# Attention, expert routing and a cosine feed-forward in fp32: where the product's hi part is made, the order of the last two steps, and hints at conditional items

## The chip, the cores and the metric

One core of a Trainium2 chip runs the whole kernel. The time is the device time of one execution in microseconds. The kernel before took 1527.83 us (median of three runs, 1527.18 to 1529.36).

## The reference

Three stages, 4608 tokens of width 512. Attention over keys and values that are mean-pooled by 8; a router that sends each token to one of 8 experts (its two matrices 512x1024 and 1024x512, relu between, scaled by the gate); then a feed-forward for all tokens with one pair of matrices, 512x2048 and 2048x512. The part that the change touches most is the last:

```
def _moe2_ref(x, w_in, w_out):
    h = x @ w_in
    g = h * np.cos(h)
    return (g @ w_out).astype(np.float32)
```

## The kernel before

Matrix products keep fp32 accuracy with operands split in two: hi is the value rounded to the matmul's format, lo is the rest, and each product is the sum of three, hi by hi, lo by hi and hi by lo.

**Order.** Everything stands under a manual schedule: each engine does its instructions in the order in which the program lists them, and waits only for the data and buffers of each instruction.

**Expert items.** An expert's tokens are done in items of 512 (wide) or 256 (narrow). Five wide items are always there. Up to seven more wide ones and up to eight narrow ones depend on the routing: `more_wide(i)` opens `tc.If(nw > i)`, issues the item and nests the next one in it, `more_narrow(j)` does the same with `nn > j`. So each chain ends with one branch past the items that are not there, on every engine, after which an engine runs the code behind the chain. In the profile these branches are at L1037 and L1064. In an item `gemm1` (L788) makes eight blocks of 12 matmuls, in two PSUM banks by turns, each emptied by a relu on ScalarE (L791) and a lo part on VectorE (L792); `gemm2` (L803) makes the second product. Between them ScalarE (L127, `w_hi`) and GpSimd or VectorE (L130, `w_lo`) split the expert's weights. `t_x` (L773 to L776) transposes and splits the next item's x. SyncE loads weights and rows and stores the result (`y_store`, L811). The first narrow item also prepares the feed-forward (`prepare`): it loads and splits the first three weight tiles.

**Feed-forward.** 9 groups g of 512 tokens, 16 slices f of 128 hidden units: 144 steps n = 16 g + f. Step n lists, in this order:

- in group 0 only, for f up to 12: `f_split(n + 3)`, the split of the weight tile of three steps later, hi by ScalarE (L916), lo by GpSimd (L917); the load of the tile of six steps later;
- `ff1(n)`: 12 matmuls into one of three PSUM banks (L941);
- at f = 14 and 15: `x2_split`, half of the next group's x each, hi by ScalarE (L926), lo by GpSimd (L927);
- `ff2(n - 2)`: 12 matmuls (L965), into four banks that hold the group's output of 4 tiles of 128 tokens; after f = 15 `store`, four copies out of PSUM (L971 VectorE, L973 ScalarE) and then four scattered sends by GpSimd (L976);
- `act(n)`: h cos(h) from the bank of ff1(n). L949 on ScalarE scales h into u; L950 and L951 on VectorE take off whole turns (L950 reads and writes SBUF, L951 has two inputs in SBUF); L952 on ScalarE is the sine; L953 on VectorE multiplies u by h; L954 on VectorE makes the hi part, L955 on VectorE the lo part.

```
nc.vector.tensor_tensor(u, u, p, ALU.mult)
nc.vector.tensor_copy(gh, u)
nc.vector.tensor_tensor(gl, u, gh.bitcast(F32), ALU.subtract)
```

Here u lies in SBUF and p, the bank of ff1, in PSUM. u, gh and gl have two buffers each, by n % 2. The last two turns of the loop (n = 144 and 145) hold only ff2(142) and ff2(143), and then the last store.

Of the kernel before, what the change touches and what calls it, by code (L numbers as in the profile page):

```python
# [8 lines left out]
F32 = mybir.dt.float32  # L9
# [4 lines left out]
AF = mybir.ActivationFunctionType  # L14
ALU = mybir.AluOpType
# [4 lines left out]
ENGINES = ET.PE, ET.DVE, ET.SP, ET.Activation, ET.Pool  # L20
# [3 lines left out]
def attention_moe_ffn_kernel(  # L24
# [13 lines left out]
    nc = tc.nc  # L38
# [3 lines left out]
    NT, DM = out.shape  # L42
    E = w1.shape[0]
# [4 lines left out]
    FC2 = F2 // 128  # L48
# [3 lines left out]
    NW0, NWM = (NT - 256 * E + 511) // 512, (NT + 255 * E) // 512  # L52
# [16 lines left out]
    def bank(i, name):  # L69
        return psp[0].tile([128, 512], F32, tag=f"p{i}", name=name)  # L70
# [24 lines left out]
    POS = const.tile([128, NTILE], I32, name="POS")  # L95
# [15 lines left out]
    xr = [wap.tile([128, XW], F32, name=f"xr{r}") for r in range(4)]  # L111
# [20 lines left out]
    def apart(group, dma):  # L132

        tc.declare_no_dep(dma.ins, group=group, reason="disjoint rows")
        tc.add_to_no_dep_group(group, dma.ins)
# [601 lines left out]
    def experts_and_feed_forward():  # L737
# [79 lines left out]
        def item(i, w, conv=None, mid=None, when=None):  # L817

            n = w // 128
            w1c, w2c, on_dve, gates, txs, (at2, at1) = when  # L820
            if i:
                pos_store(i, w)
            for k in range(16):
                if k < 8:
                    gemm1(k, w)
                else:
                    gemm2(k // 2 - 4, k % 2, w)
                    for r in txs.get(k, ()):
                        t_x(r, n)
                if mid:  # L830
                    mid(k)
                for c in (w2c if k < 8 else w1c).get(k, ()):
                    w_hi(c)
                    w_lo(c, nc.vector if c in on_dve else nc.gpsimd)
                if k == at2:
                    fetch(tab, i + 1, 5, 1)
                if k == at1:
                    fetch(tab, i + 2, 5, 0)
                if conv:
                    conv(k)  # L840
                for r in gates.get(k, ()):
                    gate(r)
            x_load(tab, i + 2, n)
            y_store(i, w)
# [43 lines left out]
        def conv_part(i, k0, k1):  # L888

            if i >= len(PART):  # L890
                return None
            j0, n = sum(PART[:i]), 7 * PART[i]
            g = (x for j in range(j0, j0 + PART[i]) for x in conv_one(j))

            def some(k):
                for _ in range(n * (k - k0 + 1) // (k1 - k0) - n * (k - k0) // (k1 - k0) if k0 <= k < k1 else 0):
                    next(g)
            return some

        NG = NTILE // 4  # L900
# [4 lines left out]
        def wf(f, s, out):  # L905
            return WF[f][s][:, out * 512:(out + 1) * 512]
# [4 lines left out]
        def f_load(f):  # L911
            nc.sync.dma_start(stage(f), wd[:, f])

        def f_split(f, eng=nc.gpsimd):
            hi, lo = WF[f]
            nc.scalar.activation(hi, stage(f), AF.Copy)  # L916
            eng.tensor_tensor(lo, stage(f), hi.bitcast(F32), ALU.subtract)  # L917

        def x2_load(g):
            nc.sync.dma_start(craw[0].rearrange("p a (b n) -> p (a b) n", b=2), yv[:, :, g * 512:(g + 1) * 512])  # L920
            nc.sync.dma_start(POSF[:, g * 4:(g + 1) * 4], pv[0, g * 512:(g + 1) * 512].rearrange("(r p) -> p r", p=128))

        def x2_split(g, k):
            raw = craw[0][:, k, :].rearrange("p (b n) -> p b n", b=2)
            x, s, t = X2[g % 2], slice(k * 2, k * 2 + 2), slice(KC + k * 2, KC + k * 2 + 2)
            nc.scalar.activation(x[:, s, :], raw, AF.Copy)  # L926
            nc.gpsimd.tensor_tensor(x[:, t, :], raw, x[:, s, :].bitcast(F32), ALU.subtract)  # L927
            if k:
                nc.gpsimd.tensor_copy(POS[:, g * 4:(g + 1) * 4], POSF[:, g * 4:(g + 1) * 4])

        PH, G, O = {}, {}, {}
        GT2 = [XHI[:, 2 * i:2 * i + 2, :] for i in range(2)]

        def ff1(n):
            g, f = seq[n]
            x2 = X2[g % 2]
            p = bank((6, 1, 7)[n % 3], "ph2")
            c = 0
            for s, m in ((0, 0), (1, 0), (0, 1)):
                for kk in range(KC):  # L940
                    nc.tensor.matmul(p, wf(f, s, 0)[:, kk * 128:(kk + 1) * 128], x2[:, m * KC + kk, :], start=(c == 0), stop=(c == 3 * KC - 1))  # L941
                    c += 1
            PH[n] = p

        def act(n):
            p = PH.pop(n)
            u, nr = ys[:, n % 2, :], co[n % 2]
            gh, gl = GT2[n % 2][:, 0, :], GT2[n % 2][:, 1, :]
            nc.scalar.activation(u, p, AF.Identity, scale=1.0 / TWO_PI_EXACT, bias=quarter)  # L949
            nc.vector.tensor_scalar(nr, u, MAGIC, MAGIC, op0=ALU.add, op1=ALU.subtract)  # L950
            nc.vector.tensor_tensor(u, u, nr, ALU.subtract)  # L951
            nc.scalar.activation(u, u, AF.Sin, scale=TWO_PI)  # L952
            nc.vector.tensor_tensor(u, u, p, ALU.mult)  # L953
            nc.vector.tensor_copy(gh, u)  # L954
            nc.vector.tensor_tensor(gl, u, gh.bitcast(F32), ALU.subtract)  # L955
            G[n] = (gh, gl)

        def ff2(n):
            g, f = seq[n]
            gh, gl = G.pop(n)  # L960
            if f == 0:
                O[g] = [bank((0, 2, 3, 4)[r], "po") for r in range(4)]
            for r in range(4):
                for c, (a, s) in enumerate(((gh, 0), (gl, 0), (gh, 1))):
                    nc.tensor.matmul(O[g][r], a[:, r * 128:(r + 1) * 128], wf(f, s, 1), start=(f == 0 and c == 0), stop=(f == FC2 - 1 and c == 2))  # L965

        def store(g):
            os = [xr[r][:, 0:DM] for r in range(4)]
            for r, o in enumerate(os):
                if r % 2:  # L970
                    nc.vector.tensor_copy(o, O[g][r])  # L971
                else:
                    nc.scalar.activation(o, O[g][r], AF.Copy)  # L973
            for r, o in enumerate(os):
                nc.gpsimd.engine_nop()  # L975
                apart("out_rows", nc.gpsimd.indirect_dma_start(  # L976
                    out=out, out_offset=bass.IndirectOffsetOnAxis(ap=POS[:, g * 4 + r:g * 4 + r + 1], axis=0),
                    in_=o, in_offset=None,
                ))
            O.pop(g)  # L980

        class Bank:
            def __init__(self, p, at):
# [49 lines left out]
        nw = nc.values_load(tot[0:1, 0:1], engines=ENGINES, min_val=NW0, max_val=NWM)  # L1033
        nn = nc.values_load(tot[0:1, 1:2], engines=ENGINES, min_val=0, max_val=E)

        def more_wide(i):
            with tc.If(nw > i) as c:  # L1037
                item(i, 512, conv_part(i, 0, 16), None, WIDE)
                if i + 1 < NWM:
                    more_wide(i + 1)  # L1040
            if i < len(PART):
                with c.Else():
                    for j in range(i, len(PART)):
                        conv_part(j, 0, 1)(0)
# [16 lines left out]
                    f_load(f)  # L1061

        def more_narrow(j):
            with tc.If(nn > j) as c:  # L1064
                item(NROW + j, 256, None, None if j else prepare, NARROW)
                if j + 1 < E:
                    more_narrow(j + 1)
            if not j:
                with c.Else():
                    for k in range(16):  # L1070
                        prepare(k)

        more_wide(NW0)
        more_narrow(0)

        rawes.close()
# [3 lines left out]
        WF.append(tuple(XLO[:, 2 * i:2 * i + 2, :].rearrange("p a n -> p (a n)") for i in range(2)))  # L1080
        seq = [(g, f) for g in range(NG) for f in range(FC2)]
        NS = len(seq)
        for n in range(NS + 2):
            if n + 3 < FC2:
                f_split(n + 3)
                if n + 6 < FC2:
                    f_load(n + 6)
            if n < NS:
                g, f = seq[n]
                ff1(n)  # L1090
                if g + 1 < NG:
                    if f == 13:
                        x2_load(g + 1)
                    if f >= 14:
                        x2_split(g + 1, f - 14)
            if n >= 2:
                ff2(n - 2)
                if seq[n - 2][1] == FC2 - 1:
                    store(seq[n - 2][0])
            if n < NS:  # L1100
                act(n)

    with tc.manual_schedule():
        with ExitStack() as xes:
# [54 lines left out]
```

## Time and profile before

| | |
|---|---|
| median of three runs | 1527.83 us |
| the profiled execution | 1523.01 us |
| its span, first to last instruction | 1521.3 us |
| mean granted TensorE clock | 0.983 of 2.4 GHz |
| busy TensorE / VectorE / ScalarE / GpSimd | 1451.7 / 919.1 / 613.4 / 449.8 us |
| the first L941 of the feed-forward | at 718.91 us |

All times inside the kernel are counted from the first instruction of the profiled execution. In the timelines a row is one instruction, or several of one kind in a row; what ended an engine's idle time before it stands in brackets, with the length of that time. PE is TensorE, PEld its weight loads, DVE VectorE, ACT ScalarE, POOL GpSimd, SP SyncE; a q behind the name is the engine's sequencer. The tile names of the feed-forward are those of the buffers it took over: L955's `xhi<-ys,xhi` is gl from u and gh, `lo<-craw,hi` at L917 is the lo part of a weight tile.

### The profile page before, as it was taken

How to read it: one execution, taken by the hardware profiler on the slowest of the kernel's cores; microseconds unless marked ns; L12 is line 12 of the kernel's file. 1: busy time of each engine (PE TensorE's matmuls, PEld its weight loads, DVE VectorE, ACT ScalarE, POOL GpSimd, SP SyncE). 2: the span in 40 equal slices, each digit the busy share in tenths (PEclk: the TensorE clock that was granted, in tenths of full speed). 3: DMA queues.
4: the chain of work that ended last, by engine and by line, in shares of the span. 5: the costliest groups of instructions: out<-in, count | busy, mean ns of one | idle time of the engine just before them, and what ended most of it. 6: DMA issues, size and time to landing. Idle time of an engine off the chain costs nothing.

```text
span 1521.3 us, 20629 instructions
## 1 busy us (share of the span) xinstructions
PE 1451.7 (95%) x7526; PEld 1231.0 (81%) x7526; DVE 919.1 (60%) x1596; ACT 613.4 (40%) x1017; POOL 449.8 (30%) x340
## 2 busy tenths in 40 slices
PE   5999887999999998998999999999999999999997
PEld 4899766888888888998778888888888888888885
DVE  5788756676666532443787565655656565655653
ACT  5888633443443445664433232222223232222321
POOL 4668552443443533433432020110102010110201
PEclk9999889999999999999999999999999999999998
DMA  8765458667676654966221010000101000010000
GB/s 270 242 206 142 168 182 286 228 198 236 208 232 211 194 173 155 332 209 210 84 83 56 0 56 1 28 28 1 56 1 56 0 28 28 2 54 0 28 1 28
DMA packets 91327, 178.86 MB, mean 118 GB/s; under 512 B 15157, under 2 KB 34106, under 8 KB 91210
## 3 DMA queue, kind: packets, MB, share of 16 engines
q1 hardware_dynamic: 85290, 158.45, 32.7%
q0 software_dynamic: 5760, 18.92, 3.4%
q8 instruction: 63, 1.03, 0.3%
q14 instruction: 54, 0.44, 0.1%
q10 hardware_dynamic: 160, 0.02, 0.0%
HBM read 136.93 MB, written 40.44 MB: 117 GB/s over the span
## 4 chain that ended last, share of the span: by engine, by line
PE 42%; issue 5%; DVE 4%; ACT 1%; POOL 0%; DVEq 0%; POOLq 0%; ACTq 0%
PE ph L941 21%; PE po L965 21%; DVE xhi L955 2%; DVE ys L951 1%; DVE ys L953 1%; ACT ys L952 1%; POOL out_dram L976 0%; DVE xhi L954 0%; DVE co L950 0%; ACT ys L949 0%; DVEq L954 0%; POOLq L975 0%; DVEq L955 0%; POOLq L976 0%; POOLq L1154 0%
## 5 line engine op out<-in xcount | busy, mean ns | idle before, releaser
L130 POOL TENSOR_TENSOR lo<-raw,hi 128x1024 fp32r<-128x1024 f32 x83 | 200.1, 2416 | 289.8 <-ACT hi L127 243.0
L949 ACT ACTIVATE ys<-ph,quarter 128x512 f32<-128x512 f32 x144 | 99.0, 688 | 298.6 <-PE ph L941 298.6
L952 ACT ACTIVATE ys<-ys 128x512 f32<-128x512 f32 x144 | 91.0, 632 | 224.5 <-DVE ys L951 224.4
L965 PE MATMUL po<-hi,xhi 128*128 128x512 f32 x576 | 179.8, 391 | 0.2
L955 DVE TENSOR_TENSOR xhi<-ys,xhi 128x512 fp32r<-128x512 f32 x144 | 157.6, 1095 | 5.1
L953 DVE TENSOR_TENSOR ys<-ys,ph 128x512 f32<-128x512 f32 x144 | 99.1, 688 | 100.5 <-ACT ys L952 100.5
L950 DVE TENSOR_SCALAR co<-ys 128x512 f32<-128x512 f32 x144 | 61.1, 425 | 159.6 <-ACT ys L949 159.6
L965 PE MATMUL po<-fh,xhi 128*128 128x512 f32 x504 | 156.4, 390 | 1.0 <-DVE xhi L955 0.9
L803 PE MATMUL py<-ha,hi 128*128 128x256 f32 (+1 forms) x576 | 140.9, 337 | 0.0
L965 PEld LDWEIGHTS po<-hi,xhi 128*128 128x128 f32 x576 | 108.1, 188 | 25.9 <-DVE xhi L955 3.6
L127 ACT ACTIVATE hi<-raw 128x1024 fp32r<-128x1024 f32 x108 | 113.1, 1053 | 1.4 <-DMA raw<-in_moe_w_dram 0.9
L965 PEld LDWEIGHTS po<-fh,xhi 128*128 128x128 f32 x504 | 94.6, 188 | 22.2 <-DVE xhi L955 2.7
L965 PE MATMUL po<-lo,xhi 128*128 128x512 f32 x288 | 112.2, 390 | 0.0
L788 PE MATMUL ph<-xhi,hi 128*128 128x512 f32 (+1 forms) x416 | 97.4, 357 | 9.6 <-ACT xhi L775 5.1
L803 PEld LDWEIGHTS py<-ha,hi 128*128 128x128 f32 x576 | 96.7, 191 | 9.7
L951 DVE TENSOR_TENSOR ys<-ys,co 128x512 f32<-128x512 f32 x144 | 99.7, 692 | 5.0
L927 POOL TENSOR_TENSOR hb<-craw,hb 128x1024 fp32r<-128x1024 f32 x10 | 24.5, 2459 | 264.1 <-ACT hb L926 264.1
L965 PE MATMUL po<-fl,xhi 128*128 128x512 f32 x252 | 98.2, 390 | 0.0
L803 PE MATMUL py<-ha,lo 128*128 128x256 f32 (+1 forms) x288 | 95.7, 332 | 0.0
L788 PE MATMUL ph<-xlo,hi 128*128 128x512 f32 (+1 forms) x416 | 94.8, 350 | 0.3 <-DVE xlo L776 0.3
L788 PE MATMUL ph<-xhi,lo 128*128 128x512 f32 (+1 forms) x416 | 94.6, 350 | 0.0
L776 DVE TENSOR_TENSOR xlo<-ptx,xhi 128x512 fp32r<-128x512 f32 x46 | 31.6, 689 | 102.6 <-ACT xhi L775 102.5
(233 smaller groups left out, 2903.8 us busy)
## 6 DMA issues: line engine op xcount, KB each, us to landing
raw<-in_moe_w_dram SPq DMA_DIRECT2D x116, 512.0 KB, 6.1
xr<-xv SPq DMA_DIRECT2D x50, 257.0 KB, 3.4
kraw<-in_k_dram SPq DMA_DIRECT2D x12, 768.0 KB, 10.5
vraw<-in_v_dram SPq DMA_DIRECT2D x8, 1152.0 KB, 7.2
craw<-yv SPq DMA_DIRECT2D x9, 1024.0 KB, 5.4
q<-in_q_dram SPq DMA_DIRECT2D x8, 1024.0 KB, 11.8
craw<-in_moe_w_in_dram SPq DMA_DIRECT2D x16, 512.0 KB, 4.4
craw<-in_moe_w_out_dram SPq DMA_DIRECT2D x16, 512.0 KB, 4.0
```

The lines of the kernel that those rows point to most:

```text
L127: nc.scalar.activation(HI[c], RAW[c], AF.Copy)
L130: eng.tensor_tensor(LO[c], RAW[c], HI[c].bitcast(F32), ALU.subtract)
L788: nc.tensor.matmul(p[:, 0:w], W[kk][:, f * 128:(f + 1) * 128], x[:, kk, 0:w], start=(c == 0), stop=(c == 3 * KC - 1))
L803: nc.tensor.matmul(p[:, 0:w], W[4 + f // 2][:, o:o + 128], h_at(f, m, w), start=(f == 0 and c == 0), stop=(f == FC1 - 1 and c == 2))
L941: nc.tensor.matmul(p, wf(f, s, 0)[:, kk * 128:(kk + 1) * 128], x2[:, m * KC + kk, :], start=(c == 0), stop=(c == 3 * KC - 1))
L949: nc.scalar.activation(u, p, AF.Identity, scale=1.0 / TWO_PI_EXACT, bias=quarter)
L950: nc.vector.tensor_scalar(nr, u, MAGIC, MAGIC, op0=ALU.add, op1=ALU.subtract)
L951: nc.vector.tensor_tensor(u, u, nr, ALU.subtract)
L952: nc.scalar.activation(u, u, AF.Sin, scale=TWO_PI)
L953: nc.vector.tensor_tensor(u, u, p, ALU.mult)
L955: nc.vector.tensor_tensor(gl, u, gh.bitcast(F32), ALU.subtract)
L965: nc.tensor.matmul(O[g][r], a[:, r * 128:(r + 1) * 128], wf(f, s, 1), start=(f == 0 and c == 0), stop=(f == FC2 - 1 and c == 2))
```

## The change

In `act` the product goes back into ff1's PSUM bank, the hi part is a copy by ScalarE from that bank, and the lo part reads the bank. The last two steps of the loop are replaced by `finish`, which goes through step 142 and 143 tile by tile, with one tile of step 142 ahead; each tile is copied out in two halves, by ScalarE and VectorE, and sent at once. Each conditional item gets a label, and each item sets, as its first instruction on all five engines, a hint for the branch of the next one, with the condition as its value.

```diff
@@ act
-            nc.vector.tensor_tensor(u, u, p, ALU.mult)
-            nc.vector.tensor_copy(gh, u)
-            nc.vector.tensor_tensor(gl, u, gh.bitcast(F32), ALU.subtract)
+            nc.vector.tensor_tensor(p, u, p, ALU.mult)
+            nc.scalar.activation(gh, p, AF.Copy)
+            nc.vector.tensor_tensor(gl, p, gh.bitcast(F32), ALU.subtract)
@@ new: one tile of ff2, one send, the last two steps
+        def ff2_tile(g, f, r, gh, gl):
+            for c, (a, s) in enumerate(((gh, 0), (gl, 0), (gh, 1))):
+                nc.tensor.matmul(O[g][r], a[:, r * 128:(r + 1) * 128], wf(f, s, 1), start=(f == 0 and c == 0), stop=(f == FC2 - 1 and c == 2))
+
+        def finish(n):
+            g, f = seq[n]
+            two = [G.pop(n - 1), G.pop(n)]
+            h = DM // 2
+            ff2_tile(g, f - 1, 0, *two[0])
+            for r in range(4):
+                if r < 3:
+                    ff2_tile(g, f - 1, r + 1, *two[0])
+                ff2_tile(g, f, r, *two[1])
+                o = xr[r][:, 0:DM]
+                nc.scalar.activation(o[:, 0:h], O[g][r][:, 0:h], AF.Copy)
+                nc.vector.tensor_copy(o[:, h:DM], O[g][r][:, h:DM])
+                send(g, r, o)
@@ more_wide, and the same in more_narrow with n{j} and nn
-            with tc.If(nw > i) as c:
+            with tc.If(nw > i, label=f"w{i}") as c:
+                if i + 1 < NWM:
+                    tc.mark_branch_hint_location(f"w{i + 1}", hint=(nw > i + 1), engines=ENGINES)
@@ the loop over the steps
-        for n in range(NS + 2):
+        for n in range(NS):
...
-            if n < NS:
-                act(n)
+            act(n)
+        finish(NS - 1)
```

## Rows read from the trace of the kernel before

**Rows 1.** Windows: length, then busy PE, PEld, DVE, ACT, POOL, clock, DMA, GB/s
```profile
740.00:760.00 20.00, 19.88 (x85) 15.23 (x83) 17.39 (x16) 6.69 (x10) 9.61 (x4) 1.00 0.27 80
...
900.00:1000.00 100.00, 100.00 (x443) 82.86 (x442) 59.68 (x96) 28.50 (x43) 13.85 (x11) 1.00 0.09 32
...
588.35:591.65 3.30, 3.30 (x15) 3.30 (x16) 0.00 (x0) 0.28 (x1) 0.00 (x0) 0.50 0.60 222
```

**Rows 2.** Chain that ended last, one block: start, us, what
```profile
1004.36 2.72 PE ph L941 x12
```

**Rows 3.** Timeline of group 0, one step: start, us, engine, line, operation
```profile
738.06 0.63 ACT L952 ACTIVATE ys<-ys 128x512 f32<-128x512 f32 x1 [3.62 <-DVE ys L951]
738.60 1.05 ACT L916 ACTIVATE hi<-ys 128x1024 fp32r<-128x1024 f32 x1
738.73 0.69 DVE L953 TENSOR_TENSOR ys<-ys,ph 128x512 f32<-128x512 f32 x1 [0.70 <-ACT ys L952]
739.52 0.43 DVE L954 CAST xhi<-ys 128x512 fp32r<-128x512 f32 x1
739.55 0.67 ACT L949 ACTIVATE ys<-ph,quarter 128x512 f32<-128x512 f32 x1
739.73 2.47 POOL L917 TENSOR_TENSOR lo<-ys,hi 128x1024 fp32r<-128x1024 f32 x1 [3.31 <-ACT hi L916]
739.98 2.76 DVE L955 TENSOR_TENSOR xhi<-ys,xhi 128x512 fp32r<-128x512 f32 x1
...
742.67 0.41 DVE L950 TENSOR_SCALAR co<-ys 128x512 f32<-128x512 f32 x1
743.12 0.69 DVE L951 TENSOR_TENSOR ys<-ys,co 128x512 f32<-128x512 f32 x1
743.84 0.63 ACT L952 ACTIVATE ys<-ys 128x512 f32<-128x512 f32 x1 [3.62 <-DVE ys L951]
```

**Rows 4.** Timeline, start of the feed-forward
```profile
718.91 2.08 PE L941 MATMUL ph<-hb,fh 128*128 128x512 f32 x4 [4.50 <-ACTq L1064]
...
721.96 1.06 ACT L916 ACTIVATE hi<-ys 128x1024 fp32r<-128x1024 f32 x1 [7.06 <-SPq L1064]
...
723.09 2.37 POOL L917 TENSOR_TENSOR lo<-ys,hi 128x1024 fp32r<-128x1024 f32 x1 [11.06 <-ACT hi L916]
...
725.21 0.54 DVE L950 TENSOR_SCALAR co<-ys 128x512 f32<-128x512 f32 x1 [11.50 <-ACT ys L949]
...
726.51 0.63 ACT L952 ACTIVATE ys<-ys 128x512 f32<-128x512 f32 x1
```

**Rows 5.** Timeline of TensorE, first block of ff1(16)
```profile
808.36 1.07 PE L941 MATMUL ph<-ha,fh 128*128 128x512 f32 x4
```

**Rows 6.** Source lines L776, L775: count, duration ns least/median/most
```profile
L776 DVE TENSOR_TENSOR xlo<-ptx,xhi x46: 677/692/692, 197.8 to 713.0; 128x512 fp32r<-128x512 f32 x46
...
L775 ACT ACTIVATE xhi<-ptx x46: 577/593/600, 197.2 to 711.5; 128x512 fp32r<-128x512 f32 x46
```

**Rows 7.** First end of a chain: its branch by source line, then timeline
```profile
L1037 PEldq COMPARE_BRANCH  x5: 65/92/3977, 441.6 to 585.3; - x5
...
588.35 1.22 PE L788 MATMUL ph<-xhi,hi 128*128 128x256 f32 x4 [3.61 <-ACTq L1037]
...
592.22 1.06 ACT L127 ACTIVATE hi<-raw 128x1024 fp32r<-128x1024 f32 x1 [0.47 <-SPq L1037]
...
594.23 0.65 PE L788 MATMUL ph<-xhi,hi 128*128 128x256 f32 x4
```

**Rows 8.** Timeline of the tail
```profile
1502.16 0.69 ACT L949 ACTIVATE ys<-ph,quarter 128x512 f32<-128x512 f32 x1 [2.90 <-PE ph L941]
...
1508.33 0.60 ACT L973 ACTIVATE xr<-po 128x512 f32<-128x512 f32 x1 [3.63 <-PE po L965]
...
1510.32 0.69 DVE L971 COPY xr<-po 128x512 f32<-128x512 f32 x1 [0.67 <-PE po L965]
...
1513.52 0.97 POOL L976 DMA_INDIRECT out_dram<-xr,POS  x1 [0.30 <-issue]
```

More of the change, by code (lines that the diff above doesn't have):

```diff
@@ L963, in ff2, with send @@
             for r in range(4):
-                for c, (a, s) in enumerate(((gh, 0), (gl, 0), (gh, 1))):
-                    nc.tensor.matmul(O[g][r], a[:, r * 128:(r + 1) * 128], wf(f, s, 1), start=(f == 0 and c == 0), stop=(f == FC2 - 1 and c == 2))
+                ff2_tile(g, f, r, gh, gl)
+        def ff2_tile(g, f, r, gh, gl):
+            for c, (a, s) in enumerate(((gh, 0), (gl, 0), (gh, 1))):
+                nc.tensor.matmul(O[g][r], a[:, r * 128:(r + 1) * 128], wf(f, s, 1), start=(f == 0 and c == 0), stop=(f == FC2 - 1 and c == 2))
+        def send(g, r, o):
+            nc.gpsimd.engine_nop()
+            apart("out_rows", nc.gpsimd.indirect_dma_start(
+                out=out, out_offset=bass.IndirectOffsetOnAxis(ap=POS[:, g * 4 + r:g * 4 + r + 1], axis=0),
+                in_=o, in_offset=None,
+            ))
         def store(g):
@@ L974, in store @@
             for r, o in enumerate(os):
[L975 to L979, printed above, removed]
-            O.pop(g)
+                send(g, r, o)
+            O.pop(g)
+        def finish(n):
[10 more added lines that the diff above has]
+                nc.vector.tensor_copy(o[:, h:DM], O[g][r][:, h:DM])
+                send(g, r, o)
         class Bank:
@@ L1063, in more_narrow @@
         def more_narrow(j):
-            with tc.If(nn > j) as c:
+            with tc.If(nn > j, label=f"n{j}") as c:
+                if j + 1 < E:
+                    tc.mark_branch_hint_location(f"n{j + 1}", hint=(nn > j + 1), engines=ENGINES)
                 item(NROW + j, 256, None, None if j else prepare, NARROW)
@@ L1087, in experts_and_feed_forward @@
                     f_load(n + 6)
-            if n < NS:
[L1089 to L1095, printed above, removed]
+            g, f = seq[n]
+            ff1(n)
+            if g + 1 < NG:
+                if f == 13:
+                    x2_load(g + 1)
+                if f >= 14:
+                    x2_split(g + 1, f - 14)
             if n >= 2:
@@ L1099, in experts_and_feed_forward @@
                     store(seq[n - 2][0])
-            if n < NS:
-                act(n)
+            act(n)
+        finish(NS - 1)
     with tc.manual_schedule():
```

## The prediction

> **What bounds the kernel now.** I read the page's busy shares, then the chain of waits, then busy times by stretch, then timelines of the places that the diff touches. In the steady feed-forward TensorE is busy 100 us of 100, VectorE 59.68 [rows 1], and the chain is nothing but blocks of 12 matmuls, 2.72 us each [rows 2]: a step has two, 5.44 us. Nothing that VectorE or ScalarE saves there can show. In group 0 it is otherwise: from 740 to 760 us VectorE is busy 17.39 of 20 [rows 1], and the reader should see why in the timeline of one step [rows 3]. ScalarE's L952 starts at 738.06 and again at 743.84, 5.78 us later, longer than 5.44, so TensorE follows a loop of the other engines: L952, ScalarE's hi part of the weight split (L916), GpSimd's lo part (L917, 739.73 to 742.20), then VectorE's L955, which started 0.25 us after GpSimd, took 2.76 us and ended 0.54 us after it, then L950, L951 and the next L952. L955 stood still while GpSimd ran. The loop holds from L952 of step 0 at 726.51 [rows 4]: the one at 743.84 is step 3's, (743.84 - 726.51) / 3 = 5.78.
>
> The other losses that the diff touches are the two places where a conditional chain ends (TensorE idle 3.61 us before 588.35 and 4.50 us before 718.91 [rows 4, 7]) and the tail.
>
> **The product in PSUM, hi part by ScalarE.** Of 144 steps those of group 0 matter first. VectorE loses L954 (0.43 us); L953 now writes PSUM, which I leave at 0.69; L955 now reads one operand from PSUM. L776 has those operands: 46 times, 677 to 692 ns, never longer [rows 6], though GpSimd's split ran beside that stage too. So L955 will be 0.69 us and no longer held. ScalarE gains a copy from PSUM: L775, 593 ns [rows 6].
>
> But that copy stands in ScalarE's order between L952 of this step and L916 of the next, and it waits for VectorE's L953. Behind it wait the split's hi part, hence GpSimd's lo part, and L949 of the next step. Counted from the start of L952, with the gaps of [rows 3]: L953 starts at 0.67 and ends at 1.36; the copy starts at 1.39; ScalarE's next instruction starts about 0.10 before the end of the one ahead (L916 at 738.60, with L952 ending at 738.69), so L916 runs 1.89 to 2.94; GpSimd 3.01 to 5.41 (2.40 taken, between the 2.37 of [rows 4] and the 2.47 of [rows 3]); L949 of the next step 2.84 to 3.53. L950 could start at 3.56, in the middle of GpSimd's run, and L951 behind it. In the kernel before neither met GpSimd in the loop, because L955 was queued ahead of them and took the whole wait.
>
> Are they held? L951 has both inputs in SBUF, as L955 had: surely, by [rows 3]. For L950 one row tells: at 725.21 it ran into GpSimd's 723.09 to 725.46 and took 0.54 instead of 0.41, ending 0.29 us after GpSimd [rows 3, 4]. L955 (0.69 alone) ended 0.54 after it, L950 (0.43 alone) 0.29: both have some 0.15 us done before they stop. So L950 ends at 5.41 + 0.29 = 5.70, L951 runs 5.73 to 6.42 and L952 starts at 6.46. The loop is 6.46 us long, not 5.78. If only L951 is held it ends at 5.41 + 0.54 and the loop is 6.00; if neither, L952 could start at 4.75 and TensorE's 5.44 would rule, (5.44 - 5.78) × 12 = -4 us for the group. I take 6.46, by the one row that shows L950 beside GpSimd.
>
> The Trainium skill ("SBUF — State Buffer", "SBUF: two separate sides") says the same as a rule: VectorE's second port pair is GpSimd's too and is held for a whole instruction, by operations with two SBUF inputs and by those that read one SBUF tensor through both ports. The trace agrees at L955 (2.76 us), and by that rule L950 and L951 are both held, the 6.46 case; an operand in PSUM frees L953 and L955 only.
>
> The start of the loop stays. L952 of step 0 is late because L916 waits until 721.96 for SyncE's code at the end of the chain, GpSimd follows until 725.46, and L950 is held by that [rows 4]; the change has the same order there. So L952 of step 12 comes at 726.51 + 12 × 6.46 = 804.0. From step 13 there are no weight splits, but two splits of the next x, at f = 14 and 15, on the same engines. Step 13 has its L952 at 807.9; the copy of that step, the x split's hi part (810.9) and GpSimd (813.3) hold step 14's L950 to 813.6, L952 comes at 814.4, the second hi part ends at 817.3 and GpSimd's second lo part at 819.8. TensorE, whose ff2(12) has its second matmul at 806.75 (L955's end 2.71 after L952), would reach ff1(16) at 815.0; its last two matmuls need that lo part, so it ends at 820.3. Before it began at 808.36 [rows 5], hence ended at 811.08. Group 0 costs **+9.2 us**; with only L951 held the same count gives 814.3, +3.2 us. Later groups have the two x splits only. There a step's chain from L949 to L955 takes 4.7 us by the lengths above, while ff2(n) starts four blocks, 10.9 us, after ff1(n); two waits for GpSimd of some 2 us fit into the 6 us between, so nothing.
>
> **The hints.** At the first end TensorE's own branch took 3977 ns (of five, 65 at the least, 92 in the middle), then it waited for ScalarE's, until 588.35 [rows 7]. If the hint works both are there early, and ff1 of the narrow item (gemm1) starts near 585.5. But ScalarE's next weight split, L127 at 592.22, waited for SyncE [rows 7], whose join waits for its last store to land; no hint shortens that. The relu of the second block is queued behind L127 (it ends 593.28). With two PSUM banks gemm1 can do three blocks (half of 2.72 us and a little, 1.44 each: 585.5 to 589.8), then stands until about 593.8; now the fourth starts at 594.23 [rows 7]. Gain 0.4 us. And after the idle 3.61 us the granted clock was 0.50, 1.2 GHz, for the 3.3 us to 591.65 [rows 1], four matmuls taking 1.22 us against 0.65 [rows 7]; the new idle stretch of 4 us is no shorter, so the low clock comes back behind it and loses half of such 3.3 us, 1.6. Some of that was paid before in blocks 0 to 2, which now wait anyway. I take **+0.6**, between -0.5 (no drop) and +1.7.
>
> At the second end ff1(0) could start near 715 instead of 718.91, but the loop's start is set by SyncE (721.96) as shown, so TensorE only waits later, for ff2(0) at 728.5. **0**, between -3 (SyncE also sooner) and +1. The hint instructions themselves are in no row: ten items, at most 0.1 us each by the shortest branches (65 ns), on sequencers that run ahead; 0, at most +1.
>
> The Trainium skill ("Runtime: NRT & Kernel Launch", "Instruction fetch mechanics") says that a taken branch to code outside the fetched blocks waits for a fetch. The 3977 ns agree. Taken alone it would credit the hints with both gaps and the low clock after them, some -10 us: that is a rival below.
>
> **The tail.** The last L949 starts at 1502.16 [rows 8]; with L950 to L953 at [rows 3] lengths the product is there at 1505.42, its hi part at 1506.05, L955's lo part at 1506.78. The new order lets TensorE reach the first tile of step 143 after ff2(141) and two tiles of step 142, at 1505.82, so its second matmul waits from 1506.05 to 1506.83: **+0.8**. Then the last tile ends near 1511.06, is copied in halves (0.43 taken). Sends follow each other by 1.27 us (0.97 + 0.30), and the first of the four, at 1513.52 - 3 × 1.27, came 0.78 us after its tile's copy (1508.33 + 0.60) [rows 8]. The tile before the last ends 0.68 us earlier, so its send starts 0.47 + 0.78 - 0.68 = 0.57 us after the last tile's end and the last send at 1.84, not at 3.24 (1513.52 less 1510.28, just before the copy at 1510.32): **-1.4**. After a send nothing changes. Sum **-0.6**, between 0 and -1.4.
>
> **Sum.** 9.2 + 0.6 + 0 - 0.6 = +9.2 us. The profiled execution took 1523.01 us (span 1521.3 and 1.7 around it), so 1532.2; the runs shown have a median of 1527.83, 4.8 higher, so the time that I forecast for such runs is **1537.0 us**, 0.6% slower. Its own range is 1533 (tail and ends at their best, loop 6.35) to 1541 (the clock also drops in the 2 us wait before ff1(16), +2.9, and the hints cost 1).
>
> **Rivals.** (1) *Relief works*: L950 and L951 slip past GpSimd, the loop falls below 5.44. For it: one short row only shows L950 held. Against it: L955 with the operands of L951 was held in every step. -4 - 0.6, and up to -3 at the ends: 1520 to 1523.5, faster. It decides where GpSimd's lo part no longer covers L950 and L951. (2) *Only L951 is held*: 3.2 - 0.6 = +2.6, 1530.4, no change to tell. (3) *The hints pay in full*: SyncE's join is also early, both gaps shrink to under 1 us, -2.9 and -3.8, and at least 1.6 us of low clock go behind each: -10; with the longer loop and the tail -1.4, 1526.4, no change; the wait of L127 and L916 on SyncE [rows 4, 7] is against it. (4) *The hints do nothing* (old gaps stay): 1536.4, inside the forecast.
>
> **How the numbers follow.** A difference under 0.2% (3 us) is no change here. Forecast with (4): 0.66. (2): 0.10, same. (3): 0.07, same. (1): 0.17, faster. Faster 0.17, same 0.17, slower 0.66. The range reaches down into (1), to 1522, and leaves out its lower half and what lies above 1541: 1522 to 1541.
>
> **What would show it.** Right: in group 0 L952 to L952 near 6.46 us, L950 some 2.1 us long beside L917, L955 at 0.69; ff1(16) ending some 9 us later from the chain's end; TensorE's wait before ff2 about 1 us in each step. Wrong: a period at or under 5.44, L950 at 0.43 beside GpSimd, or L127 and L916 after the ends starting earlier than SyncE's store lands. In the tail: a wait near 0.8 us at the first tile of step 143 and 1.3 us between sends.

## The result, and the profile after

The changed kernel takes 1538.2 us (median of four runs, 1537.52 to 1541.01) beside 1527.51 us for the kernel before (four runs, 1525.09 to 1529.36). The ratio is 1.0074, 95% interval 1.0055 to 1.0094: slower by 10.7 us. The forecast was 1537.0 us and slower.

The profiled execution of after took 1541.01 us (span 1539.3), the slowest of its runs, as the one of before (1523.01) was the fastest of its own. The two spans differ by 18.0 us, of which 7.2 arise ahead of the end of the wide chain, where the code of both is the same but for the hints. The hints are not the reason: the same part lasts 585.3 to 591.0 us in the traces of the six kernels without hints there, 588.1 to 592.5 in the five with them. So stages are compared here, counted from the last copy of the gate (L781, `pt<-pp 1x512`) ahead of the narrow chain: from it to the last instruction are 936.04 us before and 946.84 after, 10.8 more, close to the difference of the medians. Each stage is read from one trace of each kernel.

| stage, us | before | after |
|---|---|---|
| last wide copy L781 to the second product of the first narrow item (end of the wide chain) | 16.61 | 18.35 |
| from there to the last scaling of the chain, L807 (narrow items) | 112.64 | 111.47 |
| L807 to the first sine L952 (end of the narrow chain, start of the feed-forward) | 12.00 | 11.69 |
| first sine to the end of ff1(16) (group 0) | 84.57 | 95.46 |
| ff1(16) to the last matmul | 699.20 | 700.02 |
| last matmul to the end of the span (tail) | 11.02 | 9.85 |

Group 0 holds the loss, +10.9 us. One step of it in the timeline of after (start, us, engine, line, operation; what ended the idle time before it in brackets) answers to [rows 3]:

```profile
740.39 0.63 ACT L952 ACTIVATE ys<-ys 128x512 f32<-128x512 f32 x1 [2.91 <-DVE ys L951]
741.05 0.70 DVE L953 TENSOR_TENSOR ph<-ys,ph 128x512 f32<-128x512 f32 x1 [0.70 <-ACT ys L952]
741.78 0.60 ACT L954 ACTIVATE xhi<-ph 128x512 fp32r<-128x512 f32 x1 [0.76 <-DVE ph L953]
742.28 1.05 ACT L916 ACTIVATE hi<-craw 128x1024 fp32r<-128x1024 f32 x1
742.41 0.69 DVE L955 TENSOR_TENSOR xhi<-ph,xhi 128x512 fp32r<-128x512 f32 x1 [0.66 <-ACT xhi L954]
743.23 0.68 ACT L949 ACTIVATE ys<-ph,quarter 128x512 f32<-128x512 f32 x1
743.41 2.40 POOL L917 TENSOR_TENSOR lo<-craw,hi 128x1024 fp32r<-128x1024 f32 x1 [4.06 <-ACT hi L916]
743.94 2.15 DVE L950 TENSOR_SCALAR co<-ys 128x512 f32<-128x512 f32 x1 [0.83 <-ACT ys L949]
746.13 0.69 DVE L951 TENSOR_TENSOR ys<-ys,co 128x512 f32<-128x512 f32 x1
746.85 0.63 ACT L952 ACTIVATE ys<-ys 128x512 f32<-128x512 f32 x1 [2.95 <-DVE ys L951]
```

L955 has fallen from 2.76 to 0.69 us, as it was meant to. But L950, 0.41 us in [rows 3], now takes 2.15: it starts 0.53 us into GpSimd's L917 and ends at 746.09, 0.28 us after L917 (745.81). The wait on GpSimd has moved from L955 to L950, and since ScalarE's copy L954 stands ahead of the split L916, L917 comes later in the loop. Sine to sine is 6.46 us here, 6.50 in the mean of the 12 steps (733.97 to 812.02), beside 5.78 before. The windows (columns as in [rows 1]: length, then busy PE, PEld, DVE, ACT, POOL, clock, DMA share, GB/s), in the last one ff1(16)'s end:

```profile
740.00:760.00 20.00, 19.50 (x83) 15.26 (x82) 13.04 (x13) 8.38 (x13) 7.19 (x3) 0.98 0.30 81
900.00:1000.00 100.00, 100.00 (x443) 82.81 (x442) 50.72 (x75) 39.66 (x61) 12.45 (x9) 1.00 0.07 22
825.40:829.40 4.00, 3.95 (x10) 3.12 (x11) 2.81 (x2) 1.08 (x2) 2.70 (x2) 0.57 0.07 5
```

VectorE is 4.35 us less busy from 740 to 760 us, and the stage is slower: its busy share says nothing of the loop. In the steady part TensorE is busy 100 us of 100 in both kernels.

The start of the feed-forward in after, beside [rows 4]:

```profile
723.15 1.17 PE L941 MATMUL ph<-hb,fh 128*128 128x512 f32 x4 [0.97 <-ACTq L1086]
...
729.43 1.06 ACT L916 ACTIVATE hi<-ys 128x1024 fp32r<-128x1024 f32 x1 [6.76 <-SPq L1086]
...
730.57 2.36 POOL L917 TENSOR_TENSOR lo<-ys,hi 128x1024 fp32r<-128x1024 f32 x1 [10.77 <-ACT hi L916]
...
731.09 2.12 DVE L950 TENSOR_SCALAR co<-ys 128x512 f32<-128x512 f32 x1 [9.61 <-ACT ys L949]
...
733.97 0.63 ACT L952 ACTIVATE ys<-ys 128x512 f32<-128x512 f32 x1 [1.61 <-DVE ys L951]
...
736.01 1.52 PE L968 MATMUL po<-fh,xhi 128*128 128x512 f32 x2 [4.43 <-ACT xhi L954]
```

TensorE's idle time before ff1(0) has fallen from 4.50 to 0.97 us, and now it stands 4.43 us before ff2(0), where it did not wait before: L916 still waits for SyncE. The branches by source line (count; least, median, longest in ns; first and last start), at the end of the wide and of the narrow chain, beside [rows 7]; the first two lines are ScalarE's of before, the others of after:

```profile
L1037 ACTq COMPARE_BRANCH  x5: 34/40/50, 445.2 to 588.4; - x5
L1064 ACTq COMPARE_BRANCH  x7: 34/34/50, 588.5 to 718.9; - x7
...
L1057 PEldq COMPARE_BRANCH  x5: 68/92/387, 448.8 to 592.1; - x5
L1057 ACTq COMPARE_BRANCH  x5: 34/49/69, 452.4 to 595.2; - x5
L1057 SPq EVENT_SEMAPHORE  x9: 17/17/17, 594.5 to 598.9; - x9
...
L1086 PEldq COMPARE_BRANCH  x7: 65/68/357, 592.4 to 722.4; - x7
L1086 ACTq COMPARE_BRANCH  x7: 34/34/64, 599.3 to 722.8; - x7
L1086 SPq EVENT_SEMAPHORE  x9: 17/17/17, 725.6 to 729.4; - x9
```

TensorE's branch is 387 ns instead of 3977, but at the end of the wide chain the next work is no earlier. The timeline there:

```profile
595.16 0.74 PE L788 MATMUL ph<-xhi,hi 128*128 128x256 f32 x4 [3.22 <-ACTq L1057]
...
599.63 0.38 ACT L791 ACTIVATE ha<-ph 128x256 fp32r<-128x256 f32 x1 [6.60 <-issue]
599.91 1.05 ACT L127 ACTIVATE hi<-raw 128x1024 fp32r<-128x1024 f32 x1
...
600.52 1.11 PE L788 MATMUL ph<-xhi,hi 128*128 128x256 f32 x4 [2.23 <-DVE ha L792]
```

and the window behind the second wait (columns as above):

```profile
600.70:604.00 3.30, 3.30 (x17) 3.30 (x17) 0.57 (x2) 1.10 (x4) 2.38 (x1) 0.50 0.61 173
```

TensorE waits 3.22 us for ScalarE's end of the chain (its event came at 595.1), and a second time, 2.23 us, because ScalarE's first relu came only at 599.63. Behind it the granted clock is 0.50, and four matmuls take 1.11 us, against 0.65 at full clock [rows 7]. The branches show where ScalarE was: it passed the last branch of the wide chain (L1057) at 595.2 us and its next instruction, the first branch of the narrow chain (L1086), started at 599.3, with no wait for a semaphore between them, 4.13 us. Before, the same two branches (L1037, L1064) stood 0.12 us apart.

The tail, beside [rows 8]:

```profile
1524.56 0.69 DVE L955 TENSOR_TENSOR xhi<-ph,xhi 128x512 fp32r<-128x512 f32 x1 [0.72 <-ACT xhi L954]
1524.58 0.50 PE L968 MATMUL po<-xlo,xhi 128*128 128x512 f32 x1
1525.31 0.73 PE L968 MATMUL po<-xlo,xhi 128*128 128x512 f32 x2 [0.22 <-DVE xhi L955]
...
1527.69 0.97 POOL L972 DMA_INDIRECT out_dram<-xr,POS  x1 [76.47 <-issue]
...
1531.51 0.97 POOL L972 DMA_INDIRECT out_dram<-xr,POS  x1 [0.30 <-issue]
```

The four sends end the kernel as before, 1.27 us apart; from the last matmul to the span's end it is 1.17 us shorter.

### The profile page after: what moved, and what is told of

The parts are those of the page before. It is cut to its first block, busy times and chain, and to the rows that moved or that the text cites. A ratio compares the mean times of both kernels' runs of the same rounds, so it can differ in the third digit from the quotient of the medians.

```text
span 1539.3 us, 20848 instructions
## 1 busy us (share of the span) xinstructions
PE 1460.3 (95%) x7526; PEld 1234.5 (80%) x7526; DVE 850.0 (55%) x1454; ACT 697.4 (45%) x1163; POOL 442.4 (29%) x340
## 4 chain that ended last, share of the span: by engine, by line
PE 40%; issue 6%; DVE 4%; ACT 2%; POOL 0%; ACTq 0%; POOLq 0%
PE ph L941 20%; PE po L968 20%; DVE co L950 2%; DVE ys L951 1%; DVE ph L953 1%; ACT ys L952 1%; ACT ys L949 1%; ACT hi L916 0%; POOL out_dram L972 0%; ACT fh L916 0%; ACT ha L926 0%; ACT xhi L954 0%; ACT xlo L916 0%; DVE xr L981 0%; DVE xhi L955 0%
## 5 line engine op out<-in xcount | busy, mean ns | idle before, releaser
L950 DVE TENSOR_SCALAR co<-ys 128x512 f32<-128x512 f32 x144 | 107.1, 744 | 161.6 <-ACT ys L949 161.6
L952 ACT ACTIVATE ys<-ys 128x512 f32<-128x512 f32 x144 | 91.0, 632 | 221.2 <-DVE ys L951 221.2
L955 DVE TENSOR_TENSOR xhi<-ph,xhi 128x512 fp32r<-128x512 f32 x144 | 99.6, 692 | 104.5 <-ACT xhi L954 103.1
L949 ACT ACTIVATE ys<-ph,quarter 128x512 f32<-128x512 f32 x144 | 98.8, 686 | 128.2 <-PE ph L941 128.2
L953 DVE TENSOR_TENSOR ph<-ys,ph 128x512 f32<-128x512 f32 x144 | 100.3, 696 | 100.6 <-ACT ys L952 99.9
L954 ACT ACTIVATE xhi<-ph 128x512 fp32r<-128x512 f32 x144 | 86.2, 598 | 118.6 <-DVE ph L953 117.0
L951 DVE TENSOR_TENSOR ys<-ys,co 128x512 f32<-128x512 f32 x144 | 99.7, 692 | 5.0
```

The lines of the kernel that those rows point to most:

```text
L953: nc.vector.tensor_tensor(p, u, p, ALU.mult)
L955: nc.vector.tensor_tensor(gl, p, gh.bitcast(F32), ALU.subtract)
```

## The experiments

Each was timed beside the kernel before, whose median was 1526.8 us beside e1 to e4, 1526.3 beside e5 to e8 and 1526.4 beside e9. Sine period is the mean of 12 steps of group 0.

| | median, us | ratio to before, 95% interval | L807 to first sine | sine period | first sine to end of ff1(16) |
|---|---|---|---|---|---|
| before | 1526.3 to 1527.5 | | 12.00 | 5.78 | 84.57 |
| after | 1538.2 | 1.0074 [1.0055, 1.0094] | 11.69 | 6.50 | 95.46 |
| e1 product only | 1536.44 | 1.0072 [1.0053, 1.0090] | 12.71 | 6.51 | 94.59 |
| e2 hints only | 1526.4 | 0.9997 [0.9986, 1.0008] | 11.74 | 5.78 | 84.53 |
| e3 last steps only | 1524.61 | 0.9993 [0.9983, 1.0003] | 12.45 | 5.78 | 84.52 |
| e4 after, u in PSUM | 1519.97 | 0.9950 [0.9936, 0.9964] | 10.07 | 5.16 | 81.30 |
| e5 hi part by VectorE | 1520.04 | 0.9953 [0.9936, 0.9969] | 12.94 | 5.10 | 79.47 |
| e6 after, split by VectorE | 1521.85 | 0.9955 [0.9939, 0.9972] | 10.87 | 5.35 | 80.64 |
| e7 e4 without hints | 1519.95 | 0.9955 [0.9938, 0.9972] | 11.38 | 5.00 | 79.19 |
| e8 e7, narrow hints, other order | 1522.07 | 0.9969 [0.9952, 0.9986] | 12.32 | 5.00 | 79.19 |
| e9 e4, other order | 1516.94 | 0.9932 [0.9910, 0.9954] | 8.52 | 4.99 | 78.84 |

**e1_product_only**: the kernel before with the three lines of `act` alone.

```diff
-            nc.vector.tensor_tensor(u, u, p, ALU.mult)
-            nc.vector.tensor_copy(gh, u)
-            nc.vector.tensor_tensor(gl, u, gh.bitcast(F32), ALU.subtract)
+            nc.vector.tensor_tensor(p, u, p, ALU.mult)
+            nc.scalar.activation(gh, p, AF.Copy)
+            nc.vector.tensor_tensor(gl, p, gh.bitcast(F32), ALU.subtract)
```

> The kernel before with the change in act alone: product in the PSUM bank, hi part by ScalarE, lo part from the bank. Theory A (the copy stands ahead of the weight split in ScalarE's order, so GpSimd's lo part now meets L950 and L951 and holds them): L952 to L952 6.5 us in group 0, from L952 of step 0 to the end of ff1(16) about 95 us against 84.6 before, so 10 to 11 us slower than before, about 1538. Rival (the loss sits in the hints or the tail): 84 or less, the time of before or 4 us less.

Measured 1536.44 us, 9.7 over the kernel before. The same loop is there:

```profile
745.25 2.39 POOL L917 TENSOR_TENSOR lo<-ys,hi 128x1024 fp32r<-128x1024 f32 x1 [4.12 <-ACT hi L916]
745.79 2.15 DVE L950 TENSOR_SCALAR co<-ys 128x512 f32<-128x512 f32 x1 [0.83 <-ACT ys L949]
```

The three lines by themselves make the loss: the ratio is 1.0072, beside 1.0074 for the whole change.

**e2_hints_only**: before with labels and hints alone (the diff shows the wide chain; the narrow one has the same).

```diff
-            with tc.If(nw > i) as c:
+            with tc.If(nw > i, label=f"w{i}") as c:
+                if i + 1 < NWM:
+                    tc.mark_branch_hint_location(f"w{i + 1}", hint=(nw > i + 1), engines=ENGINES)
```

> The kernel before with the hints alone. Theory A: TensorE's branches at the ends fall from 4 us to under 0.5, but SyncE's join sets what follows: from the last copy of the second chain (L807) to L952 of step 0 stays at 11.7 to 12.0 us, and the first end costs 1 to 2 us more than before (low clock later, ScalarE late twice); time +0 to +2 us, no change within 0.2%. Rival (the hints pay): 5 to 10 us faster. Rival (the hints are what made the changed kernel slow): 8 to 10 us slower.

Measured 1526.4 us, no difference. The gap before ff1(0) is 0.96 us, the first sine 0.26 us earlier after L807, the end of the wide chain 0.63 us longer than before (17.24 against 16.61), less than the 1 to 2 us expected.

**e3_finish_only**: before with `ff2_tile`, `send` and `finish` alone.

```diff
-        for n in range(NS + 2):
+        for n in range(NS):
...
+        finish(NS - 1)
```

> The kernel before with the last two steps by tiles alone; the product and its hi part are made as before. Theory: the last send starts 1.2 to 1.4 us sooner behind TensorE's last matmul, and the wait for the lo part of step 143 is 0.6 to 0.7 us (a cast of 0.43 in place of the 0.60 copy): 0.5 to 0.8 us faster, not to be told from no change by the times, but by the trace. Rival: the sends were not what ended last, then slower by the wait, 0.7 us.

Measured 1524.61 us; the interval of the ratio is -1.7 to +0.3 tenths of a per cent, so the times alone don't settle it. In the trace TensorE's part is 0.61 us longer (699.81 against 699.20) and the tail 1.14 shorter (9.88 against 11.02): -0.5 us.

**e4_u_in_psum**: after, with u in a free PSUM bank; the sine goes to the SBUF buffer.

```diff
-            u, nr = ys[:, n % 2, :], co[n % 2]
+            s, nr = ys[:, n % 2, :], co[n % 2]
+            u = bank(5, "pu")
...
-            nc.scalar.activation(u, u, AF.Sin, scale=TWO_PI)
-            nc.vector.tensor_tensor(p, u, p, ALU.mult)
+            nc.scalar.activation(s, u, AF.Sin, scale=TWO_PI)
+            nc.vector.tensor_tensor(p, s, p, ALU.mult)
```

> The changed kernel, and u (the scaled h) kept in the free PSUM bank 5, the sine written to SBUF: L950 and L951 then read PSUM, everything else, GpSimd's work and ScalarE's order with it, is as in the changed kernel. Theory A (L950 and L951 are held by GpSimd, because both their inputs lie in SBUF or are read through both ports): L950 and L951 0.7 us each beside GpSimd, the loop 5.0, so TensorE's 5.44 rules in group 0; from L952 of step 0 to the end of ff1(16) 76 to 79 us, L952 of step 0 1.5 us sooner; 16 to 20 us faster than the changed kernel, 1519 to 1522. Rival (the copy costs as one more link in the loop or by ScalarE's load, whatever holds L950): 6.0 us or more per step, no faster than the kernel before.

Measured 1519.97 us, 18 faster than after by the medians, with the same copy by ScalarE in the same place. Its timeline (L950 to L956 are after's L949 to L955):

```profile
748.26 2.40 POOL L917 TENSOR_TENSOR lo<-craw,hi 128x1024 fp32r<-128x1024 f32 x1 [2.61 <-ACT hi L916]
748.76 0.69 DVE L951 TENSOR_SCALAR co<-pu 128x512 f32<-128x512 f32 x1 [0.80 <-ACT pu L950]
749.49 0.70 DVE L952 TENSOR_TENSOR pu<-pu,co 128x512 f32<-128x512 f32 x1
750.22 0.60 ACT L953 ACTIVATE ys<-pu 128x512 f32<-128x512 f32 x1 [1.49 <-DVE pu L952]
```

Both operations lie inside GpSimd's run and take 0.69 and 0.70 us. The turn removal that stood on GpSimd with its operand in SBUF (2.15 us) does not with it in PSUM, though alone it is slower (0.69 against 0.42). The period is 5.0 us in the first seven steps, below the 5.44 us that TensorE needs for its two blocks [rows 2], and 5.44 in the last four. From the first sine to the end of ff1(16) it is 81.30 us, not the 76 to 79 expected; e7 shows why.

**e5_hi_on_vector**: before with the product in PSUM, the hi part still VectorE's.

```diff
-            nc.vector.tensor_tensor(u, u, p, ALU.mult)
-            nc.vector.tensor_copy(gh, u)
-            nc.vector.tensor_tensor(gl, u, gh.bitcast(F32), ALU.subtract)
+            nc.vector.tensor_tensor(p, u, p, ALU.mult)
+            nc.vector.tensor_copy(gh, p)
+            nc.vector.tensor_tensor(gl, p, gh.bitcast(F32), ALU.subtract)
```

> The kernel before with the product in the PSUM bank, but the hi part still made by VectorE (from the bank): ScalarE's order stays that of the kernel before, sine, then weight split. Theory A (it is the copy's place ahead of the split that moves GpSimd onto L950 and L951; the product in PSUM frees L955): L953, L954 and L955 run beside GpSimd unheld, 0.69 each, L950 comes when GpSimd is nearly done and is held to its end; loop 5.1 us, so TensorE's 5.44 rules; from L952 of step 0 to the end of ff1(16) 76 to 80 us; 4 to 7 us faster than before, 1520 to 1523. Rival (the product in PSUM itself costs, by VectorE's writes to the bank): slower than before, as the product alone was.

Measured 1520.04 us. Beside e1 only the engine of the copy differs, and that makes 16 us:

```profile
750.33 1.04 ACT L916 ACTIVATE hi<-craw 128x1024 fp32r<-128x1024 f32 x1
...
751.25 0.69 DVE L954 CAST xhi<-ph 128x512 fp32r<-128x512 f32 x1
...
751.45 2.40 POOL L917 TENSOR_TENSOR lo<-craw,hi 128x1024 fp32r<-128x1024 f32 x1 [2.70 <-ACT hi L916]
...
752.59 1.54 DVE L950 TENSOR_SCALAR co<-ys 128x512 f32<-128x512 f32 x1
```

Here L916 follows the sine at once, so GpSimd starts 1.66 us after the sine (749.79) instead of 3.02. L950 is still held, to 754.13, 0.28 us after L917's end, but that end comes earlier, and the period is 5.10 us. So both the hold and the place of the split in ScalarE's order are needed for the loss.

**e6_split_on_vector**: after with `f_split(n + 3, nc.vector)`: GpSimd has no part in the loop.

> The changed kernel with the lo part of the weight split in group 0 made by VectorE instead of GpSimd; ScalarE's order with the copy ahead of the split stays. Theory A (what costs is the port that GpSimd holds): L950 back to 0.43, loop 5.4, even though VectorE has 1.23 us more per step; from L952 of step 0 to the end of ff1(16) 77 to 83 us; 10 to 16 us faster than the changed kernel, 1522 to 1528. Rival (a longer loop because of the copy and a fuller VectorE): 6 us per step or more, no faster than the changed kernel.

Measured 1521.85 us. With no GpSimd beside it L950 is 0.42 us, and the split itself is 1.22 on VectorE; group 0 is as expected (80.64 us), the time just under the forecast range:

```profile
749.81 1.22 DVE L917 TENSOR_TENSOR lo<-craw,hi 128x1024 fp32r<-128x1024 f32 x1 [0.26 <-ACT hi L916]
750.95 0.42 DVE L950 TENSOR_SCALAR co<-ys 128x512 f32<-128x512 f32 x1
```

**e7_finish_u**: e4 without the hints. It tests whether they help once the loop is short.

> The kernel before with the product and u in PSUM, the hi part by ScalarE, and the last two steps by tiles; no hints. Theory: TensorE is the limit from ff2(0) on; against before -5 us in group 0 and -0.5 in the tail, about 1521, and within 1 us of the same kernel with hints, as the hints alone made no difference. Rival (the hints help once the loop no longer follows SyncE): 3 us or more slower than the one with them.

Measured 1519.95 us, as e4: the hints are worth nothing there either. The windows of e4 and of e7 (in this order) show what becomes of their gain:

```profile
731.60:738.30 6.70, 5.97 (x13) 4.42 (x14) 3.52 (x6) 4.37 (x7) 2.44 (x2) 0.50 0.50 135
731.60:738.30 6.70, 6.70 (x31) 5.53 (x31) 3.87 (x6) 4.01 (x6) 2.40 (x1) 1.00 0.44 115
```

With hints ff2(0) starts 12.1 us after L807, without them 14.4. But in e4 TensorE stood 2.79 us before ff2(0), and from 731.6 to 738.3 us its granted clock was 0.50; e7 has no such wait and full clock there. The 28 blocks from ff2(0) to the end of ff1(16) take 79.3 us in e4 and 76.2 in e7, so the 2.3 us are lost again.

**e8_all**: e7 with hints in the narrow chain only, and the splits and loads of later steps issued behind `act(n)`, so that ScalarE's first weight split, which waits for SyncE, no longer stands ahead of the first `act`.

```diff
+                if j + 1 < E:
+                    tc.mark_branch_hint_location(f"n{j + 1}", hint=(nn > j + 1), engines=ENGINES)
...
-            if n + 3 < FC2:
-                f_split(n + 3)
...
             act(n)
+            if n + 3 < FC2:
+                f_split(n + 3)
...
```

> The kernel of e7, the hints in the narrow chain alone, and the weight split of the loop listed behind act(n) instead of ahead of ff1(n). Theory (the gain of the hint at the second end was swallowed because ScalarE's first split waits for SyncE's join, and the first act stands behind it): now act(0) no longer waits for SyncE; from the last L807 of the chain to the sine of step 0 under 7 us instead of 12, TensorE idle under 1 us at this end and not again before ff2(0); 5 to 7 us faster than e7, about 1515. Rival (something else holds the start, the load of the sine table or the weight tiles): as e7, 1521.

Measured 1522.07 us: the expectation missed. TensorE's branch was short, and ScalarE came late:

```profile
L1085 PEldq COMPARE_BRANCH  x7: 67/73/378, 591.2 to 722.2; - x7
L1085 ACTq EVENT_SEMAPHORE  x1: 17/17/17, 727.1 to 727.1; - x1
```

```profile
727.20 2.07 PE L941 MATMUL ph<-hb,fh 128*128 128x512 f32 x4 [5.15 <-ACTq L1085]
```

The narrow items also took longer, 115.19 us against 111.5 to 112.6. ScalarE's event came 4.90 us after its own branch here, against 0.39 us in the five kernels with hints on both chains and 4.27 before. Why its hint did nothing here is open.

**e9_all_hints_order**: e4 (hints on both chains) with the order of e8.

> e4 (the change with u in PSUM, hints at both chains) with the splits and loads of later steps issued behind act(n) instead of ahead of ff1(n). The first two steps' splits were done before the chain, so TensorE and ScalarE need nothing of SyncE for steps 0 to 2. Theory (the start of the feed-forward was held by ScalarE's split of step 3 standing ahead of Identity(0) and waiting for SyncE's store, about 6 us, a wait that the hints alone can't remove): from the last narrow item's scaling L807 to the first sine 5 to 7 us instead of 10.07, the whole 3 to 5 us shorter than e4: 1515 to 1517.5 us beside a before of 1526.5. Rival (the store's landing is still needed before step 3, and the loop of 12 steps catches up on it: the 12-step stretch grows by what the start gains; or ScalarE fetches late again as with hints on the narrow chain alone): as e4, 1519.5 to 1521.

Measured 1516.94 us, in the forecast range of its theory. The first sine comes 8.52 us after L807, not 5 to 7: the split no longer holds it, but ScalarE's table load of the sine is put down to SyncE as well. The code gives a reason, which no run tests: the sine of step 0 writes the part of `ys` that the last item's `y_store` sends out.

```profile
721.63 0.66 ACT L950 ACTIVATE pu<-ph,quarter 128x512 f32<-128x512 f32 x1 [3.57 <-PE ph L941]
724.90 1.28 ACT L953 ACT_TABLE_LOAD   x1 [2.61 <-SPq L1087]
726.20 0.60 ACT L953 ACTIVATE ys<-pu 128x512 f32<-128x512 f32 x1
```

From ff2(0) at 728.21 to the end of ff1(16) at 805.04 are 76.8 us, and the 28 blocks that TensorE does in it take 28 × 2.72 = 76.2: in group 0 TensorE is now the bound, as in e5, e7 and e8 (76.2 each). TensorE's longest waits at the start are 0.97 and 1.23 us, and the clock stays at 1.00. So of the 3.0 us to e4, e9 gains 1.55 before the first sine and 2.46 in group 0, and loses 1.0 at the end of the wide chain. e9 is faster than before by 9.4 us and than after by some 21 (by the medians), and has the lowest median, though its interval overlaps those of e4 and e7.

## Why the prediction was right

**Group 0, forecast +9.2, measured +10.9.** The step that carried it held in each detail: L955 free at 0.69; the copy ahead of the split; L917 2.40; L950 2.15 us long (2.14 taken) and ending 0.28 after GpSimd (0.29 taken); the loop 6.42 to 6.52 (6.46 taken). That it is this hold, not the extra work on ScalarE, is shown from three sides: e4 takes away the SBUF operand, e6 takes away GpSimd, e5 takes away the later start, and each alone wins the loss back and more, while ScalarE does the same copy in e4 and e6. The rival "only L951 is held" falls with L950's 2.15 us.

The missing 1.7 us are two small terms. The loop is 0.04 us longer per step, 0.5 in 12, so that the x split's second hi part came 0.6 us late. And the end of ff1(16) came 1.0 us later behind the x split's hi part than forecast, for TensorE stood 1.92 us there and its last ten matmuls ran from 825.45 to 829.43 at a mean granted clock of 0.57 (window above): 3.98 us where ten take 2.27 at full clock. The low clock behind that wait stood in the text as the upper end of the range, not in the sum. It did not come each time: in e1 the same wait, 1.93 us, was followed by full clock,

```profile
820.80:824.00 3.20, 2.84 (x11) 2.06 (x12) 2.60 (x2) 0.54 (x1) 2.72 (x2) 1.00 0.00 0
```

and there group 0 took 94.59 us, 10.0 more than before, against the forecast of 9.2.

The Trainium skill ("SBUF — State Buffer", "SBUF: two separate sides") says that VectorE's second port pair is shared with GpSimd and held for a whole instruction, by operations with two SBUF inputs and by those that read one through both ports. The traces agree: 2.15 us for the one-input L950 beside GpSimd, 0.42 without it (e6), and no hold with its operand in PSUM (e4).

**End of the wide chain, forecast +0.6, measured +1.7 (e2: +0.6).** TensorE's branch was shortened as the change says, but the rest failed: ScalarE was not early, so the gap stayed (3.22 after 3.61), and its relu 4.5 us behind it brought a second wait with low clock. It ended at the bound given, but by another way than forecast. The text took SyncE's store for the one thing that hints can't move; here ScalarE was another. The traces of the other kernels bear this out. ScalarE's event comes 2.4 to 3.4 us after its own branch in all eleven, with hints or without. The hole between its last branch of this chain and its next instruction is 4.1 to 4.5 us in the five kernels with hints here (after, e2, e4, e6, e9) and 0.12 in the six without, and the stage takes 17.1 to 18.5 us against 16.0 to 16.6. In e2 and e4 (17.2, 17.1) the granted clock was at 0.50 already in the first blocks, ahead of the second wait of 1.1 us; in the other three (18.1 to 18.5) they ran at full clock, the second wait was 2.2 to 2.4 us, and the 0.50 came behind it. The text also counted ten hinted items; the profile shows eight hints on each engine, of 28 to 54 ns.

**Start of the feed-forward, forecast 0, measured -0.3.** TensorE began ff1 3.5 us sooner and then waited 4.43 us before ff2(0), since L916 stood on SyncE. The -0.3 is within the spread: before, e1, e3 and e5, without hints, have 12.00 to 12.94 here. The rival "the hints pay in full" falls with e2. That the order of L916 held the start is borne out in part by e9, which has the hints and the last steps of e4 and gains 1.55 us there; the 2.61 us before its table load show that SyncE holds more than L916. e8 says nothing on this, since ScalarE was late there.

**Steady part and tail, forecast -0.6, measured -0.35 (e3: -0.5).** The waits at the first tile of step 143 cost 0.6 to 0.8 (0.8 taken), the sends won 1.1 to 1.2 (1.4 taken). Later groups: as forecast nothing. L950 is held there too at the x splits, but ff1(16) to the last matmul is 699.21 us in e1, 699.20 before.

**The sum.** +1.74 (end of the wide chain) -1.17 (narrow items) -0.31 (start) +10.89 (group 0) +0.82 -1.17 (last steps and tail) = +10.80 us by stages, against +9.2. The narrow items vary by as much between kernels that share their code (111.46 in e3, 112.64 before), so those -1.17 are not put down to the change. Total 1538.2 against 1537.0. That the total came so near is in part luck: the narrow items' -1.17 stands against misses of +1.7 in group 0 and +1.1 at the end of the wide chain. The way to the loss, the hold of L950 in group 0, was not luck.

The rival "relief works" was wrong of this change but right of the idea: with u in PSUM, too, the loop does fall under 5.44 us and the kernel takes 1520, where that rival stood.

## What to carry to other kernels

When an operation is freed from a shared port, look which instruction of the same engine runs beside the other user next, and where its operands lie: here the wait moved there, and was gone when that one read PSUM too (e4). Moving work to an idle engine puts it into that engine's order; count what is queued behind it, here the split whose lo part holds the port. A shorter branch on one engine gave nothing here (e2), where the next wait was for another engine's end of the same chain.

## What was not expected of the hardware

The one-input L950 on a 128x512 SBUF tile was held until 0.28 us after GpSimd's run, 2.15 us where it takes 0.42 alone. With its input in PSUM it takes 0.68 to 0.69 us in all 144 steps of e4, with or without GpSimd beside it, and so loses alone and wins in company. The hints took TensorE's taken branch from 3977 to 387 ns and from 4387 to 357 ns, and ScalarE's way from its branch to its event at the end of the narrow chain from 4.27 to 0.39 us. At the end of the wide chain that way stayed as it was, and the hole of 4.1 to 4.5 us behind ScalarE's last branch came only with the hints; in e8 ScalarE's hint at the end of the narrow chain did nothing. What ScalarE did in the hole stays open: no semaphore wait stands in it.
